# A transformer stack's score cells issued as two 64-column matmul tiles in place of one of 128 columns

## The chip, the cores and the metric

The kernel runs on one core of a Trainium2 chip. Five engines work side by side, each in its own program order, and meet through semaphores: TensorE (PE; its weight loads are listed apart as PEld), VectorE (DVE), ScalarE (ACT), GpSimd (POOL) and SyncE (SP), which issues the DMAs. TensorE multiplies a stationary operand, loaded first, by a moving one that streams through, and writes to PSUM, eight banks of 128 partitions by 512 float32. Its array can be addressed in tiles, by a `tile_position` of row and column. The metric is the device time of one execution in microseconds, the median of the runs shown.

## What is computed

Two rounds of attention and MLP over one sequence of 2048 positions and width 512, the same weights in both rounds, each with a layer norm ahead and a residual behind:

```
x = x + attention(layernorm(x))     # 32 heads of 16
x = x + mlp(layernorm(x))           # 512 -> 1792 -> 512, gelu
x = x + attention(layernorm(x))
x = x + mlp(layernorm(x))

attention: q, k, v = x @ wqkv
           p = softmax(q @ k.T / 4)           # 2048 x 2048 for each head
           (p @ v) @ wo
mlp:       gelu(x @ w1 + b1) @ w2 + b2
```

The inputs and weights are bfloat16.

## The kernel before

**Cells.** The scores are computed transposed, keys on the partitions. One score cell is 128 keys by 512 query columns: K is the stationary operand, 32 rows of it (two heads of 16) by 128 keys, and the queries are the moving one, 32 rows by 512, masked so that one head's rows count. Each cell has a row group `a` of the array (rows 32a to 32a+31) and fills one PSUM bank. There are 4096 cells over both layers. In the profile they are the matmuls of line 1598, `ps<-qp,kt 32*128 32x512`: 32 rows by 128 columns of stationary operand. `qp` holds the masked queries, `kt` K.

**Groups.** `scores` (line 1817) sends cells in groups. Two slots of PSUM banks take turns, `SLOTS = ((0, 1, 2), (3, 4))` with bank 5 (`THIRD`) joined to the second later on. In most of the program a group is three cells of different row groups: two for ACT and a third for DVE (`join`, `trade`, `attach`). A group waits until ACT (semaphore `s_act`) has read the slot's two banks, and its third cell until DVE (`s_dve`) has read its own.

**What reads them.** ACT takes the exponential of the two cells in one instruction of 128x1024 (line 2234, `exps`), to the probability tiles `pt` or to buffers lent for them (`kt`, `v`, `q`). DVE does the third cell by an exponent trick (line 1867, `dfirst`): one multiply-add to 16-bit integers; POOL (line 2097, `shift`) adds constants to them for two more copies, and the three copies enter the value product with weighted copies of V (`vc`).

**Columns.** All other matmuls of weight (`quads`, line 715, for the projections and the MLP; `pvs`, line 2301, for probabilities times values) use tiles of all 128 rows by a strip of 32 columns, four strips side by side; in the profile they read `128*32` and `128*17`. Each set of four is called a round here. PE thus goes back and forth between groups of scores on row tiles and runs of rounds on column tiles.

**The order** of each engine's work is fixed when the program is built: `_Sched` runs the kernel's generators against a table of costs (`MM`, 0.213 us for a round or a group, `SW`, 0.107 us for a change between the two shapes) and appends operations to each engine's list. It fits as many column rounds between two score groups as these costs say PE has time for, and fillers (lines 1586 and 2309) where PE would stand idle. `_Prog.group` (line 275) writes an operation's list of functions with its waits ahead and one semaphore increment on the last.

Of the kernel before, what the change touches and what calls it, by code (L numbers as in the profile page):

```python
# [704 lines left out]
class _Plan:  # L705
# [883 lines left out]
    def score(self, cell, qs, bank):  # L1589

        T = self.T
        pi, kt, a = cell
        l, seg, g = self.pas[pi][:3]
        gb = self.heads(seg, g)[0]
        lhsT = T["K"][l][32 * a:32 * a + 32, gb, kt * 128:(kt + 1) * 128]
        rhs = T["QP"][32 * a:32 * a + 32, qs, :]
        o = self.bank(bank)
        return (lambda e: e.matmul(o, lhsT=lhsT, rhs=rhs, start=True, stop=True, tile_position=(32 * a, 0)),  # L1598
                ["K%d.%d.%d" % (l, gb, kt // 4), "QP.%d" % qs] + ["K0.0.0.b"] * ((l, gb) == (0, 0) and kt in (2, 3)))

    def next_act(self, used=()):
# [820 lines left out]
```

## Time and profile before

| | us |
|---|---|
| median of 3 runs | 1374.87 (1374.37 to 1375.13) |
| profiled execution | 1374.89 |
| its span, first to last instruction | 1373.1 |
| PE busy | 1338.8 (98%) |
| PEld busy | 390.1 (28%) |
| ACT busy | 1349.0 (98%) |
| DVE busy | 1261.8 (92%) |
| POOL busy | 802.8 (58%) |

The granted TensorE clock is 1.00 throughout. A row of a group of instructions gives line, engine and operation, output and inputs by the program's names, shape and count, then busy time in us, the mean of one in ns, and the idle time ahead of it with what ended most of it. A row of a stretch in order of time gives start and length in us, then engine, line, operation and how many are merged in it. Matmul ends are modelled and follow one another closely, so the distance of starts tells more than the lengths. PE's shapes are given as rows*columns of the stationary operand, then the moving one.

### The profile page before, as it was taken

What the parts mean: (1) busy time and instruction counts of PE and PEld (TensorE: products, weight loads), DVE (VectorE), ACT (ScalarE), POOL (GpSimd) and SP (SyncE); (2) the same over time, 40 slices, a digit from 0 to 9 for tenths busy, and PEclk for the clock granted to TensorE, in tenths of its full rate; (3) what the DMA queues carried; (4) which work ended last, traced back from release to release, by engine and by line L of the source; (5) the groups of instructions that cost most, each with busy time, mean ns of one, the idle gap of its engine ahead of it and who ended that gap; (6) DMA issues with size and microseconds to landing.
All of it is one profiled execution on the core that took longest, in us unless ns stands there. A gap on an engine that the chain in (4) does not pass through costs nothing.

```text
span 1373.1 us, 42332 instructions
## 1 busy us (share of the span) xinstructions
PE 1338.8 (98%) x18168; PEld 390.1 (28%) x18168; DVE 1261.8 (92%) x2504; ACT 1349.0 (98%) x1385; POOL 802.8 (58%) x1352
## 2 busy tenths in 40 slices
PE   9999999999999999999999999999999999999999
PEld 3222222222222222222222222222222222333446
DVE  8999999989999899998979899999999898999894
ACT  7999999999999999999999999999999999999995
POOL 1367667657665567665626666546656665765461
DMA  5300000123221221112451141100104314201112
GB/s 149 72 2 1 2 2 23 49 75 97 71 43 45 89 83 55 44 51 65 114 109 40 49 128 57 48 17 12 37 24 117 93 40 143 83 14 44 29 34 83
DMA packets 122296, 80.20 MB, mean 58 GB/s; under 512 B 36732, under 2 KB 121084, under 8 KB 122108
## 3 DMA queue, kind: packets, MB, share of 16 engines
q1 hardware_dynamic: 122108, 77.49, 20.6%
q8 instruction: 143, 2.34, 0.7%
q14 instruction: 45, 0.37, 0.1%
HBM read 65.67 MB, written 4.19 MB: 51 GB/s over the span
## 4 chain that ended last, share of the span: by engine, by line
ACT 83%; PE 10%; DVE 6%; DMA 1%; issue 0%
ACT pt L2234 70%; PE ps L715 5%; ACT kt L2234 3%; ACT g L1276 3%; PE ps L1598 3%; ACT v L2234 2%; PE ps L2301 2%; DVE dp L1867 2%; ACT q L2234 2%; DVE kt L1867 1%; ACT L2234 1%; ACT L1276 1%; ACT g L2234 1%; DVE stats L848 0%; DMA wr<-in_B_w_dram 0%; DMA wr<-in_A_wqkv_dram 0%
## 5 line engine op out<-in xcount | busy, mean ns | idle before, releaser
L2234 ACT ACTIVATE pt<-ps 128x1024 bf16<-128x1024 f32 (+1 forms) x1183 | 1142.7, 1176 | 2.0 <-PE ps L1598 1.6
L1598 PE MATMUL ps<-qp,kt 32*128 32x512 bf16 x4096 | 551.5, 384 | 16.6 <-ACT pt L2234 12.2
L2097 POOL INT64_ADD dp<-dp x732 | 440.2, 613 | 204.8 <-DVE dp L1867 123.1
L1867 DVE TENSOR_SCALAR dp<-ps 128x512 uint16<-128x512 f32 x733 | 483.3, 679 | 26.3 <-PE ps L1598 23.4
L1598 PEld LDWEIGHTS ps<-qp,kt 32*128 32x128 bf16 x4096 | 138.4, 91 | 569.7 <-ACT pt L2234 466.7
L2097 POOL INT64_ADD kt<-kt x320 | 190.1, 599 | 174.1 <-DVE kt L1867 93.6
L2301 PE MATMUL ps<-pt,v 128*17 128x512 bf16 (+1 forms) x2758 | 273.9, 359 | 1.4 <-ACT pt L2234 0.7
L1867 DVE TENSOR_SCALAR kt<-ps 128x512 uint16<-128x512 f32 x309 | 207.4, 683 | 23.4 <-PE ps L1598 20.8
L2301 PE MATMUL ps<-dp,vc 128*17 128x512 bf16 (+1 forms) x1652 | 220.7, 357 | 0.6 <-POOL xf L2097 0.4
L2301 PE MATMUL ps<-dp,v 128*17 128x512 bf16 (+1 forms) x826 | 139.1, 357 | 3.4 <-DVE xt L1076 2.4
L2097 POOL INT64_ADD v<-v x155 | 94.1, 611 | 71.7 <-DVE v L1867 35.8
L715 PE MATMUL ps<-xf,wr 128*32 128x512 bf16 (+1 forms) x1888 | 134.6, 366 | 0.5 <-DVE g L1258 0.4
L2301 PE MATMUL ps<-kt,vc 128*17 128x512 bf16 (+1 forms) x766 | 117.6, 340 | 1.0 <-POOL xf L2097 0.3
L1867 DVE TENSOR_SCALAR v<-ps 128x512 uint16<-128x512 f32 x154 | 102.8, 682 | 13.2 <-PE ps L1598 12.8
L715 PE MATMUL ps<-wr,g 128*32 128x512 bf16 x1408 | 108.1, 384 | 0.5 <-DVE dp L1867 0.2
L2301 PEld LDWEIGHTS ps<-pt,v 128*17 128x17 bf16 x2758 | 69.8, 88 | 74.5 <-issue 51.8
L2301 PE MATMUL ps<-kt,v 128*17 128x512 bf16 (+1 forms) x507 | 85.8, 350 | 1.7 <-DVE xt L1076 1.0
L2097 POOL INT64_ADD xf<-xf x78 | 46.5, 596 | 65.5 <-DVE xf L1867 40.3
L1258 DVE TENSOR_SCALAR g<-ps,hb1t 128x512 bf16<-128x512 f32 (+1 forms) x112 | 78.9, 706 | 1.0 <-PE ps L715 1.0
L2301 PEld LDWEIGHTS ps<-dp,vc 128*17 128x17 bf16 x1652 | 56.7, 88 | 42.0 <-issue 24.4
L2234 ACT ACTIVATE kt<-ps 128x1024 bf16<-128x1024 f32 (+1 forms) x60 | 63.4, 1189 | 0.0
L2301 PE MATMUL ps<-v,vc 128*17 128x512 bf16 x308 | 60.8, 381 | 0.0
(124 smaller groups left out, 1425.5 us busy)
## 6 DMA issues: line engine op xcount, KB each, us to landing
wr<-in_B_w_dram SPq DMA_DIRECT2D x174, 256.0 KB, 2.9
wr<-in_A_wqkv_dram SPq DMA_DIRECT2D x24, 256.0 KB, 3.3
x<-in_A_x_dram SPq DMA_DIRECT2D x7, 512.0 KB, 4.3
wr<-in_A_wo_dram SPq DMA_DIRECT2D x10, 256.0 KB, 3.7
kept<-x SPq DMA_DIRECT2D x4, 512.0 KB, 3.1
x<-kept SPq DMA_DIRECT2D x4, 512.0 KB, 4.4
out_dram<-x SPq DMA_DIRECT2D x16, 128.0 KB, 2.5
q<-in_B_w_dram SPq DMA_DIRECT2D x3, 512.0 KB, 4.5
```

The source lines that it names most:

```text
L715: return [lambda e, a=a: e.matmul(out[32 * a:32 * a + 32, :], lhsT=lhsT[:, 32 * a:32 * a + 32], rhs=rhs, start=start, stop=stop, tile_posi ...
L1258: yield _Op("dve", 0.21 + n / 966, lambda e, fc=fc, pb=pb: e.tensor_scalar(T["G"][:, fc, q], pb, T["HB1T"][:, fc:fc + 1], None, op0=ALU.ad ...
L1276: lambda e, g=g: e.activation(out=g, in_=g, func=ACT.Gelu_apprx_tanh), reads=gk, writes=gk, prio=2)
L1598: return (lambda e: e.matmul(o, lhsT=lhsT, rhs=rhs, start=True, stop=True, tile_position=(32 * a, 0)), ["K%d.%d.%d" % (l, gb, kt // 4), "Q ...
L1867: yield _Op("dve", 0.682, lambda e: e.tensor_scalar(u, self.bank(b), E_SCALE, E_BIAS, op0=ALU.mult, op1=ALU.add), reads=["B.%d" % b], writ ...
L2097: op = _Op("pool", PFIX + PWORD * 128 * (hi - lo), lambda e: e.int64_add(dst, src, by * PACKED), reads=reads, writes=writes)
L2234: yield _Op("act", EXPC + 0.4267 * n, lambda e, src=src, dst=dst: e.activation(out=dst, in_=src, func=ACT.Exp, scale=0.25), reads=["B.%d" ...
L2301: op.fns.append(lambda e, o=o, lhsT=q[0][0][m], rhs=q[0][1][:, n * m:n * m + n], a=a, st=st, sp=sp: e.matmul(o, lhsT=lhsT, rhs=rhs, start= ...
```

## The change

Each score cell's matmul of 32 rows by 128 columns is issued as two of 32 rows by 64 columns, one for the first 64 keys and one for the second. Both stream the same 32x512 queries, stand on the same row group, at columns 0 and 64, and write the lower and upper 64 partitions of the same bank. The cell's two matmuls stand one behind the other in the place of the one; the planner's costs are the same and so is its order.

```
     def score(self, cell, qs, bank):
...
         lhsT = T["K"][l][32 * a:32 * a + 32, gb, kt * 128:(kt + 1) * 128]
         rhs = T["QP"][32 * a:32 * a + 32, qs, :]
         o = self.bank(bank)
-        return (lambda e: e.matmul(o, lhsT=lhsT, rhs=rhs, start=True, stop=True, tile_position=(32 * a, 0)),
+        return (lambda e: [e.matmul(o[64 * c:64 * c + 64, :], lhsT=lhsT[:, 64 * c:64 * c + 64], rhs=rhs, start=True, stop=True, tile_position=(32 * a, 64 * c))
+                           for c in range(2)][-1],
                 ["K%d.%d.%d" % (l, gb, kt // 4), "QP.%d" % qs] + ["K0.0.0.b"] * ((l, gb) == (0, 0) and kt in (2, 3)))
```

The lambda returns the second matmul, so a semaphore increment that the cell had goes on that one. Lines below 1598 move down by one.

On PE in the first layer's attention, at the place that the prediction follows in time (413.89 us and on), before (columns x moving columns, count, and the semaphores waited for; `pt`, `dp`, `v` and `xp` hold probabilities, `wr` weights):

```order
2741 L1598 MATMUL ps<-qp,kt 128x512 [waits s_act]
2742 L1598 MATMUL ps<-qp,kt 128x512
2743 L1598 MATMUL ps<-qp,kt 128x512 [waits s_dve]
2744 L715 MATMUL ps<-xf,wr 32x512 x4
2745 L2301 MATMUL ps<-v,vc 17x512 [waits s_pool]
2746 L2301 MATMUL ps<-v,vc 17x512
2747 L2301 MATMUL ps<-dp,vc 17x512 x2
2748 L2301 MATMUL ps<-xp,v 17x512 [waits s_pool,s_dve]
2749 L2301 MATMUL ps<-xp,v 17x512
2750 L2301 MATMUL ps<-dp,vc 17x512 x2
2751 L1598 MATMUL ps<-qp,kt 128x512 [waits s_act]
2752 L1598 MATMUL ps<-qp,kt 128x512 x2
```

The same place on PE now:

```order
3090 L1598 MATMUL ps<-qp,kt 64x512 [waits s_act]
3091 L1598 MATMUL ps<-qp,kt 64x512 x3
3092 L1598 MATMUL ps<-qp,kt 64x512 [waits s_dve]
3093 L1598 MATMUL ps<-qp,kt 64x512
3094 L715 MATMUL ps<-xf,wr 32x512 x4
3095 L2302 MATMUL ps<-v,vc 17x512 [waits s_pool]
3096 L2302 MATMUL ps<-v,vc 17x512
3097 L2302 MATMUL ps<-dp,vc 17x512 x2
3098 L2302 MATMUL ps<-xp,v 17x512 [waits s_pool,s_dve]
3099 L2302 MATMUL ps<-xp,v 17x512
3100 L2302 MATMUL ps<-dp,vc 17x512 x2
3101 L1598 MATMUL ps<-qp,kt 64x512 [waits s_act]
3102 L1598 MATMUL ps<-qp,kt 64x512 x5
```

Three score matmuls have become six, the wait for ACT ahead of the first and that for DVE ahead of the third cell's first half; the twelve column matmuls between, their order and their waits are what they were.

ACT, which waits for these groups (the exponentials, from an earlier place in the first layer's attention), before:

```order
156 L2234 ACTIVATE pt<-ps 128x2x512 [waits s_pe] x6
157 L2234 ACTIVATE pt<-ps 128x1024 [waits s_pe] x8
158 L2234 ACTIVATE pt<-ps 128x2x512 [waits s_pe]
159 L2234 ACTIVATE kt<-ps 128x2x512 [waits s_pe]
160 L2234 ACTIVATE pt<-ps 128x2x512 [waits s_pe] x2
```

And now:

```order
156 L2235 ACTIVATE pt<-ps 128x2x512 [waits s_pe] x6
157 L2235 ACTIVATE pt<-ps 128x1024 [waits s_pe] x8
158 L2235 ACTIVATE pt<-ps 128x2x512 [waits s_pe]
159 L2235 ACTIVATE kt<-ps 128x2x512 [waits s_pe]
160 L2235 ACTIVATE pt<-ps 128x2x512 [waits s_pe] x2
```

Only the line number has moved.

More of the change, by code (lines that the diff above doesn't have):

```diff
@@ L1597, in score @@
         o = self.bank(bank)
-        return (lambda e: e.matmul(o, lhsT=lhsT, rhs=rhs, start=True, stop=True, tile_position=(32 * a, 0)),
+        return (lambda e: [e.matmul(o[64 * c:64 * c + 64, :], lhsT=lhsT[:, 64 * c:64 * c + 64], rhs=rhs, start=True, stop=True, tile_position=(32 * a, 64 * c))
+                           for c in range(2)][-1],
                 ["K%d.%d.%d" % (l, gb, kt // 4), "QP.%d" % qs] + ["K0.0.0.b"] * ((l, gb) == (0, 0) and kt in (2, 3)))
```

## The prediction

> **What bounds the kernel now.** I read the page's busy times and its chain first, then the groups, then one stretch of attention in order of time, on PE and on ACT, and last the durations by line that price the edit.
>
> From the page (busy us, share, instructions; then the chain by engine and by line):
>
> ```profile
> PE 1338.8 (98%) x18168; PEld 390.1 (28%) x18168; DVE 1261.8 (92%) x2504; ACT 1349.0 (98%) x1385; POOL 802.8 (58%) x1352
> ...
> ACT 83%; PE 10%; DVE 6%; DMA 1%; issue 0%
> ...
> L2234 ACT ACTIVATE pt<-ps 128x1024 bf16<-128x1024 f32 (+1 forms) x1183 | 1142.7, 1176 | 2.0 <-PE ps L1598 1.6
> L1598 PE MATMUL ps<-qp,kt 32*128 32x512 bf16 x4096 | 551.5, 384 | 16.6 <-ACT pt L2234 12.2
> ```
>
> Two engines stand at 98%, and the chain runs mostly through ACT's exponentials. PE's busy share says little, because matmuls overlap and their ends are modelled; what PE has to spare must be read from the spacing of its starts. PE in the middle of attention (start, length, count; the first five rows are score groups with the columns' work between them left out):
>
> ```profile
> 408.55 0.39 PE L1598 MATMUL ps<-qp,kt 32*128 32x512 bf16 x3
> ...
> 409.42 0.39 PE L1598 MATMUL ps<-qp,kt 32*128 32x512 bf16 x3
> ...
> 410.29 0.39 PE L1598 MATMUL ps<-qp,kt 32*128 32x512 bf16 x3
> ...
> 411.23 0.39 PE L1598 MATMUL ps<-qp,kt 32*128 32x512 bf16 x3
> ...
> 412.09 0.39 PE L1598 MATMUL ps<-qp,kt 32*128 32x512 bf16 x3
> ...
> 412.99 0.39 PE L1598 MATMUL ps<-qp,kt 32*128 32x512 bf16 x3
> 413.31 0.61 PE L715 MATMUL ps<-xf,wr 128*32 128x512 bf16 x8
> 413.89 0.39 PE L1598 MATMUL ps<-qp,kt 32*128 32x512 bf16 x3
> 414.21 0.40 PE L715 MATMUL ps<-xf,wr 128*32 128x512 bf16 x4
> 414.43 0.38 PE L2301 MATMUL ps<-v,vc 128*17 128x512 bf16 x2
> 414.44 0.38 PE L2301 MATMUL ps<-dp,vc 128*17 128x512 bf16 x2
> 414.65 0.38 PE L2301 MATMUL ps<-xp,v 128*17 128x512 bf16 x2
> 414.66 0.38 PE L2301 MATMUL ps<-dp,vc 128*17 128x512 bf16 x2
> 414.97 0.39 PE L1598 MATMUL ps<-qp,kt 32*128 32x512 bf16 x3
> 415.29 0.39 PE L2301 MATMUL ps<-xp,vc 128*17 128x512 bf16 x2
> 415.30 0.39 PE L2301 MATMUL ps<-pt,v 128*17 128x512 bf16 x2
> 415.72 0.39 PE L1598 MATMUL ps<-qp,kt 32*128 32x512 bf16 x3
> 416.04 0.83 PE L715 MATMUL ps<-xf,wr 128*32 128x512 bf16 x12
> 416.81 0.39 PE L1598 MATMUL ps<-qp,kt 32*128 32x512 bf16 x3
> ```
>
> Three cells go out together, and 0.32 us later (414.97 to 415.29) comes column work, four matmuls side by side in a round of 0.22 us (414.21, 414.43, 414.65). From the last round to the next scores it is again 0.31 to 0.32 (414.66 to 414.97). So each change between the two shapes costs about 0.10 us above a round, and the least a group can take is 0.63 us with one round of columns, 0.85 with two, 1.07 with three. From 408.55 to 416.81 stand nine groups with 19 rounds (two in each of the first six, then three, one and three): least 9 x 0.63 + 10 x 0.22 = 7.87 us, taken 8.26. PE idles 0.39 us, 43 ns per group or 4.7%. That idling sits in four places: 410.29 to 411.23 (0.94, least 0.85), 412.09 to 412.99 and 412.99 to 413.89 (0.90 each), and 414.97 to 415.72 (0.75, least 0.63). There PE waits until ACT frees the slot.
>
> The exponentials that these groups feed (start, length; ACT's rows overlap, so the step is from start to start):
>
> ```profile
> 413.52 1.23 ACT L2234 ACTIVATE pt<-ps 128x1024 bf16<-128x1024 f32 x1
> ...
> 414.42 1.24 ACT L2234 ACTIVATE pt<-ps 128x1024 bf16<-128x1024 f32 x1
> ...
> 415.40 1.18 ACT L2234 ACTIVATE pt<-ps 128x1024 bf16<-128x1024 f32 x1
> ...
> 416.32 2.09 ACT L2234 ACTIVATE pt<-ps 128x1024 bf16<-128x1024 f32 x2
> ```
>
> ACT's own step is 0.90 us (413.52 to 414.42). A score group's matmuls end 0.39 us after it starts, so the scores of 412.99 and 413.89 lay ready 0.14 us before ACT took them, but those of 414.97 ended at 415.36 and ACT started at 415.40: it had been waiting, and its step was 0.98. The second of the last row starts at about 416.32 + 2.09 - 1.18 = 417.23, right behind the scores of 416.81 (ended 417.20): late again. So ACT leads the chain, but with 0.04 to 0.2 us between it and PE, and twice in nine steps PE is already the later one, each time behind a group with three rounds.
>
> **The change, part by part.** Every score group issues six pairs of weight load and matmul in place of three; the cells are 4096, three to a group as in the rows above, so 4096 / 3 = 1365 groups. The order on PE, DVE, ACT, POOL and SP is otherwise as it was, with the same waits at the same places and one increment per group of matmuls as before. No DMA, no wait and no other engine's instruction is added, so the whole cost is PE time. Durations by line (ns: least, median, longest) of the 128-column load and its matmul, of 32-column ones and of 17-column ones, and PE in one window (busy us, count, then PEld):
>
> ```profile
> L1598 PEld LDWEIGHTS ps<-qp,kt x4096: 90/91/94, 11.8 to 1342.8; 32*128 32x128 bf16 x196
> L1598 PE MATMUL ps<-qp,kt x4096: 371/385/386, 11.8 to 1342.8; 32*128 32x512 bf16 x196
> ...
> L715 PEld LDWEIGHTS ps<-xp,wr x512: 92/94/97, 361.1 to 877.4; 128*32 128x32 bf16 x171
> L715 PE MATMUL ps<-xp,wr x512: 379/379/391, 361.1 to 877.6; 128*32 128x512 bf16 x171
> ...
> L2301 PEld LDWEIGHTS ps<-pt,v x2758: 86/88/93, 15.6 to 1345.5; 128*17 128x17 bf16 x197
> L2301 PE MATMUL ps<-pt,v x2758: 272/379/387, 15.6 to 1345.6; 128*17 128x512 bf16 x156, 128*17 128x256 bf16 x41
> ...
> 400.00:420.00 20.00, 8.60 (x66) 2.13 (x66) 1.00 0.15 42
> ```
>
> *Three more pairs.* In the window 66 score loads, 22 groups, cover 2.13 us: 97 ns per group. One load is 91, so the second and third add 6 together, 3 ns each. Three more pairs: 9 ns per group.
>
> *Narrower loads.* A 64-column load isn't in the trace. Between 17 and 32 columns the load goes from 88 to 94 ns, 0.4 per column, and the longest matmul, the one that follows a load it had to wait for, from 387 to 391, against 379 in steady rounds. On that line 128 columns would take 132 ns; they take 91. So the whole-width load is a quicker kind, and 64 columns on the line of the narrow ones take 94 + 32 x 0.4 = 107 ns, 16 more than now; by the matmuls, 391 + 32 x 0.27 = 400 against 385, 15 more. From above: if the loads of the two halves of a row group followed each other, the second would add what a 64-column load shows of itself, 400 - 379 = 21, so 37. From below: the load shows 385 - 379 = 6 ns now, and no more than these 6 can go. I take 17, nearest the two lines.
>
> *Switching between shapes.* There are as many as now, 0.10 us each, and the trace has the same price into scores (0.31) and out of them (0.32) although the shapes differ, so I put this change at nothing; the faster rival below says otherwise.
>
> *Issuing.* A dense run of short matmuls shows that PE can take more instructions than it will be given:
>
> ```profile
> 1357.42 3.23 PE L715 MATMUL ps<-xf,kt 128*32 128x256 bf16 x112
> 1360.48 0.28 PE L715 MATMUL ps<-xf,wr 128*32 128x256 bf16 x4
> ```
>
> 112 pairs start in 3.06 us, 27 ns a pair. A step of 0.9 us will hold six pairs of scores and eight of columns, 14 x 27 = 0.38 us: nothing on the path.
>
> *The sum on PE.* 9 + 17 = 26 ns per group, 35.5 us over 1365 groups; bounds 9 - 6 = 3 ns (4 us) and 9 + 37 = 46 ns (63 us).
>
> *How much of it shows.* PE has 43 ns per group to spare, but not where it is needed. A delay of PE is wiped out when PE next waits for ACT; it costs time when ACT is found waiting before that. In the stretch the last such wait before ACT's late start at 415.40 ends at 413.89. Two groups' extra, 2 x 26 ns, reach that start; the wait before 415.72 hides nothing of what ACT has lost. The groups of 415.72 and 416.81 bring 52 ns more to the start at 417.23. So 0.104 us of 8.26 shows, 1.26%. Over the stretch in which ACT is full (from about 25 to 1300 us) that is 16 us. Starts that had little to spare turn late too, and the groups before and after that stretch add at most 58 x 26 ns = 1.5 us; I take 18 in all. If nothing of it were hidden it would be 35.5. The sum stands against the profiled execution's own 1374.89 us (span 1373.1, 1.8 around it), which is the median of the runs, 1374.87, to within 0.02. Forecast: 1375 + 18 = **1393 us**.
>
> For this case's own range: 9 ns per group (64 columns load as fast as 128), shown at 18 / 35.5, gives 1365 x 9 ns x 0.5 = 6 us; 46 ns per group is more than PE's 43 to spare, and by the same ratio, raised to two thirds, gives 41. That is 1381 to 1416.
>
> One rule of the Trainium skill speaks against this: its page "TensorE: Matmul & The Clock Gate", section "LDWEIGHTS (loading the stationary operand)", says that a load takes its columns divided by 1.2 GHz, whatever the rows. By it halving the columns would shorten each load from 107 to 53 ns, PE would gain 54 - 9 = 45 ns per group, and nothing would be lost. The rows above disagree: 128 columns load in 91 ns, no longer than 32.
>
> **The rivals.**
>
> *The halves take turns (far slower).* The two tiles of a cell lie on the same 32 rows and stream the same queries. If the second's weights could load only after the first's matmul, each group would take another round: 1365 x 215 ns = 293 us and the 35 above, less at most 43 ns per group (59 us) of idling: 1375 + 269 = 1644. Against it: column rounds are four matmuls on the same 128 rows with weights of their own, and a whole round takes 0.22 us (414.21 to 414.43), so tiles that share rows do run together. What no row shows is several row groups with two column strips each. The same page, section "Part 3: Packing small matmuls — row/col tiling", says that a load overlaps running matmuls only when its row group differs; by that rule it would come out like this, but it also tells of sixteen tiles of rows and columns running side by side.
>
> *PE's idling hides all of it (same).* 26 is below 43. If the waits fell before ACT's late starts, or the price were 3 ns, the time would be 1375 to 1377. For it speaks the sum of the idling, against it that ACT waited at 415.40 and 417.23 directly behind groups that had no wait.
>
> *The switch out of scores gets cheaper (faster).* The 0.10 us at each switch may be the array running empty, and a strip of 64 columns may run empty sooner than one of 128. If half of one switch went, 50 ns, PE would gain 50 - 26 = 24 ns per group; the rival turns the sign from 26 ns on. ACT then takes back only what it loses now. By this row it loses some 15 ns per step:
>
> ```profile
> 402.58 27.75 ACT L2234 ACTIVATE pt<-ps 128x1024 bf16<-128x1024 f32 x30
> ```
>
> (27.75 - 1.18) / 29 = 0.916 us against 0.90 unhindered; 1275 us x 0.015 / 0.916 = 21, half of it 10: 1365 us. Against it: 32 rows by 128 columns and 128 by 32 switch at the same price.
>
> **How the numbers follow.** Forecast's case, both halves side by side at 3 to 46 ns per group and partly hidden: 0.81. Hidden or nearly free: 0.08, 1375 to 1377. Cheaper switch: 0.06, around 1365. Halves in turn: 0.05, around 1644. A measurement of this kernel can tell about 0.2%, 2.7 us, from no change. Slower 0.81 + 0.05 = 0.86, same 0.08, faster 0.06. The range takes the first case and the edge of the second, 1377 to 1416; outside it lie the two rare cases, the rest of the hidden one, and a small share of the first beyond its bounds.
>
> **What the profile after would show.** The score line has 8192 matmuls in groups of six, starting some 3 ns apart; their load is near 107 ns and the matmul near 400. From a score group to the next column work it is 0.34 to 0.35 us in place of 0.32, into scores still 0.31. ACT's mean step grows from 0.916 to about 0.93, its idle before the exponentials names the score line more often, and PE's waits for ACT shrink. The forecast is wrong if score to columns stays at 0.32 or falls (load or switch cheaper than thought), if it is near 0.54 (halves in turn), or if it is 0.35 and ACT's step doesn't move (all hidden).

## The result, and the profile after

The changed kernel takes 1387.87 us (median of 3 runs, 1387.74 to 1389.41) against 1374.87 before: 13.0 us more, a ratio of 1.0099 with a 95% interval of 1.0076 to 1.0121. That is slower, inside the stated range and 5 us below the forecast of 1393.

The page of the profile after (busy times, the chain by engine and by line, and the two groups that were shown of before):

```profile
PE 1358.7 (98%) x22264; PEld 418.0 (30%) x22264; DVE 1266.2 (91%) x2504; ACT 1359.9 (98%) x1385; POOL 801.2 (58%) x1352
...
PE 65%; ACT 23%; DVE 10%; issue 0%; DMA 0%; POOL 0%
...
L2235 ACT ACTIVATE pt<-ps 128x1024 bf16<-128x1024 f32 (+1 forms) x1183 | 1146.6, 1092 | 3.6 <-PE ps L1598 2.0
L1598 PE MATMUL ps<-qp,kt 32*64 32x512 bf16 x8192 | 582.8, 398 | 9.8 <-ACT pt L2235 7.1
```

The busy shares have hardly moved, and say nothing of what happened. The chain does: it ran 83% through ACT and 10% through PE, and now runs 23% through ACT and 65% through PE. PE's idle time ahead of scores fell from 16.6 to 9.8 us.

The same place on PE as in the prediction, from the group that was at 412.99 on (start, length, count):

```profile
416.55 0.41 PE L1598 MATMUL ps<-qp,kt 32*64 32x512 bf16 x6
416.89 0.61 PE L715 MATMUL ps<-xf,wr 128*32 128x512 bf16 x8
417.44 0.41 PE L1598 MATMUL ps<-qp,kt 32*64 32x512 bf16 x6
417.78 0.40 PE L715 MATMUL ps<-xf,wr 128*32 128x512 bf16 x4
418.01 0.38 PE L2302 MATMUL ps<-v,vc 128*17 128x512 bf16 x2
418.02 0.38 PE L2302 MATMUL ps<-dp,vc 128*17 128x512 bf16 x2
418.23 0.38 PE L2302 MATMUL ps<-xp,v 128*17 128x512 bf16 x2
418.23 0.38 PE L2302 MATMUL ps<-dp,vc 128*17 128x512 bf16 x2
418.55 0.41 PE L1598 MATMUL ps<-qp,kt 32*64 32x512 bf16 x6
418.89 0.39 PE L2302 MATMUL ps<-xp,vc 128*17 128x512 bf16 x2
418.90 0.39 PE L2302 MATMUL ps<-pt,v 128*17 128x512 bf16 x2
419.21 0.41 PE L1598 MATMUL ps<-qp,kt 32*64 32x512 bf16 x6
419.56 0.83 PE L715 MATMUL ps<-xf,wr 128*32 128x512 bf16 x12
420.32 0.41 PE L1598 MATMUL ps<-qp,kt 32*64 32x512 bf16 x6
```

Six matmuls go out where three did, merged in one row, and the next column work follows after 0.34 to 0.35 us where it was 0.32. Over the 1133 groups of three cells the median from the first score to the next column work (called score to columns below), from the starts in the two traces, is 345 ns now and 321 before; from the last column matmul to the next scores (the way in) it is 309 now and 312 before. So a group costs 21 ns more, 29 us over 1365 groups, of which 13 show. PE's waits have shrunk: 418.55 to 419.21 is 0.66 us, where 414.97 to 415.72 was 0.75. Added up over the traces, the way in above its 312 or 309 ns falls from 23 to 11 us, and score to columns above the least for a group of its size from 27 to 23 us; these 16 us are the part of the 29 that doesn't show.

The exponentials that belong to these groups:

```profile
417.06 1.07 ACT L2235 ACTIVATE pt<-ps 128x1024 bf16<-128x1024 f32 x1
...
417.96 1.09 ACT L2235 ACTIVATE pt<-ps 128x1024 bf16<-128x1024 f32 x1
...
419.00 1.02 ACT L2235 ACTIVATE pt<-ps 128x1024 bf16<-128x1024 f32 x1
...
419.93 1.02 ACT L2235 ACTIVATE pt<-ps 128x1024 bf16<-128x1024 f32 x1
```

Here the two executions must be read by ends, start plus length. Before, the exponentials of this place end at 413.52 + 1.23 = 414.75, 414.42 + 1.24 = 415.66 and 415.40 + 1.18 = 416.58: 0.91 and 0.92 us apart, although the last started 0.98 after the one ahead of it. ACT lost nothing there; the start was late, but its end wasn't: by the lengths of the records the instruction would otherwise have stood in ACT waiting for the one ahead. Now they end at 418.13, 419.05, 420.02 and 420.95: 0.92, 0.97 and 0.93. The one behind the group with three rounds ends some 0.06 us late (982 ns after the one ahead by the trace's unrounded times, against 917), and that is time lost.

The durations of all exponentials to `pt` by line tell how far ahead PE is (ns: least, median, longest), before:

```profile
L2234 ACT ACTIVATE pt<-ps x1183: 1017/1177/1682, 12.2 to 1339.9; 128x1024 bf16<-128x1024 f32 x180, 128x1536 bf16<-128x1536 f32 x18
```

and after:

```profile
L2235 ACT ACTIVATE pt<-ps x1183: 1018/1045/1632, 12.3 to 1352.7; 128x1024 bf16<-128x1024 f32 x180, 128x1536 bf16<-128x1536 f32 x18
```

These rows mix exponentials of 1024 and 1536 columns; the lead is read from those of 1024 alone. Between 1024-column exponentials that follow one another (1100 such pairs in either trace) one that starts after the one ahead has ended takes 1023 to 1025 ns. One that starts more than some 110 ns before that end is longer, the more so the earlier it starts, and its end stays about 917 ns behind the end ahead, the median distance in both kernels. What a record is longer than 1024 ns is therefore called its lead. Half of them had 150 ns or more of it, and now have 21 or less. Before, 148 of the 1100 started more than 935 ns after the one ahead, and 124 of these still ended within 935 ns of its end; now 211 start so late, and only 43 of them end in time. Ends more than 935 ns apart were 24, which lost 2.1 us above 917; now they are 168 and lose 14.3. The difference, 12.2 us, is nearly all of the 13.

Durations by line of the 64-column load and its matmul (ns: least, median, longest):

```profile
L1598 PEld LDWEIGHTS ps<-qp,kt x8192: 101/101/104, 11.8 to 1355.8; 32*64 32x64 bf16 x200
L1598 PE MATMUL ps<-qp,kt x8192: 371/398/400, 11.8 to 1355.8; 32*64 32x512 bf16 x200
```

The load takes 101 ns against 91 for 128 columns, the matmul behind it 398 against 385.

### The profile page after: what moved, and what is told of

It reads as the page before. It is cut to its first block, busy times and chain, and to the rows that moved or that the text cites. A ratio compares the mean times of both kernels' runs of the same rounds, so it can differ in the third digit from the quotient of the medians.

```text
span 1386.1 us, 50524 instructions
## 1 busy us (share of the span) xinstructions
PE 1358.7 (98%) x22264; PEld 418.0 (30%) x22264; DVE 1266.2 (91%) x2504; ACT 1359.9 (98%) x1385; POOL 801.2 (58%) x1352
## 4 chain that ended last, share of the span: by engine, by line
PE 65%; ACT 23%; DVE 10%; issue 0%; DMA 0%; POOL 0%
PE ps L1598 23%; ACT pt L2235 21%; PE ps L715 21%; PE ps L2302 21%; DVE dp L1868 4%; DVE kt L1868 2%; ACT g L1276 1%; DVE xt L1076 1%; DVE stats L848 1%; PE ps L1586 1%; DVE xf L1868 0%; DVE v L1868 0%; ACT kt L2235 0%; DMA xf<-xln 0%; DVE x L1134 0%
## 5 line engine op out<-in xcount | busy, mean ns | idle before, releaser
L1598 PE MATMUL ps<-qp,kt 32*64 32x512 bf16 x8192 | 582.8, 398 | 9.8 <-ACT pt L2235 7.1
L1598 PEld LDWEIGHTS ps<-qp,kt 32*64 32x64 bf16 x8192 | 166.6, 101 | 554.4 <-ACT pt L2235 440.3
L1868 DVE TENSOR_SCALAR kt<-ps 128x512 uint16<-128x512 f32 x309 | 207.8, 683 | 25.7 <-PE ps L1598 21.9
```

The source lines that it names most:

```text
L1598: return (lambda e: [e.matmul(o[64 * c:64 * c + 64, :], lhsT=lhsT[:, 64 * c:64 * c + 64], rhs=rhs, start=True, stop=True, tile_position=(3 ...
L1868: yield _Op("dve", 0.682, lambda e: e.tensor_scalar(u, self.bank(b), E_SCALE, E_BIAS, op0=ALU.mult, op1=ALU.add), reads=["B.%d" % b], writ ...
```

## The experiments

The theory after the result: the change is a price on PE alone, made of a dearer load and of more tiles, and of this price only that part shows which is left when PE's waits for ACT and the lead of the exponentials are used up. Against it stand rivals for the price (it is all in the number of instructions; or in the column strips) and for the way to the end (PE is simply the bound; or DVE's cells carry the delay). The kernel before took 1374.9 to 1375.1 us beside these runs; its own runs there lie between 1374.3 and 1377.7.

### What the price is made of

**One 64-column tile per cell.** From the ninth pass on the second tile is left out:

```
-                           for c in range(2)][-1],
+                           for c in range(1 if pi >= 8 else 2)][-1],
```

> From the ninth pass on a cell issues only its first 64-key tile and leaves the scores of its other 64 keys out (what the bank held before is read in their place), so there are as many tiles as in the kernel before, each with a 64-column load. Theory: the price is two separate terms, about 13 ns per group for the narrower load and 3.3 ns for each more tile. Then from a group's first score matmul to the next column work it is 321 + 13 = 334 ns (0.33 us), and the time is near half of the change's, about 1381 us. Rival: the 64-column load costs nothing of itself and all 24 ns come from the three more pairs, 8 each: 0.32 us and 1375.

Measured: 1378.82 us, 1.0027 times before (1.0016 to 1.0038), 2 us less than the 1381 expected. Score to columns has a median of 335 ns over the groups of three tiles, as expected. Row of that kernel's PE in time:

```profile
420.40 0.41 PE L1598 MATMUL ps<-qp,kt 32*64 32x512 bf16 x3
420.74 0.62 PE L715 MATMUL ps<-xf,wr 128*32 128x512 bf16 x8
```

Three tiles with a narrower load cost 335 against 321 ns: 14 for the load. The other 10 ns of the change are the three tiles more, 3.3 each. The rival that the instructions alone make the price is out.

**Four tiles of 32 columns.**

```
-        return (lambda e: [e.matmul(o[64 * c:64 * c + 64, :], lhsT=lhsT[:, 64 * c:64 * c + 64], rhs=rhs, start=True, stop=True, tile_position=(32 * a, 64 * c))
-                           for c in range(2)][-1],
+        return (lambda e: [e.matmul(o[32 * c:32 * c + 32, :], lhsT=lhsT[:, 32 * c:32 * c + 32], rhs=rhs, start=True, stop=True, tile_position=(32 * a, 32 * c))
+                           for c in range(4)][-1],
```

> Each cell as four tiles of 32 rows by 32 columns. Theory: load 6.5 ns cheaper than with 64 columns (94 against 101), but twelve pairs in place of six at 3.3 ns: score to columns 345 - 6.5 + 20 = 358 ns (0.36 us), 34 ns more per group than before with 3 back on the way in, 47 us on PE, and 1395 to 1405 us. Rival (only the load's width counts): about 0.34 us and 1382. Rival (column strips of one row group take turns when there are four of them): over 0.5 us and above 1600.

Measured: 1397.13 us, 1.0161 (1.0146 to 1.0177), within the time expected; score to columns 351 ns, not 358. The durations by line of this kernel and a group of it on PE in time:

```profile
L1598 PEld LDWEIGHTS ps<-qp,kt x16384: 86/87/92, 11.8 to 1364.7; 32*32 32x32 bf16 x200
L1598 PE MATMUL ps<-qp,kt x16384: 372/385/387, 11.8 to 1364.7; 32*32 32x512 bf16 x200
```

```profile
412.54 0.42 PE L1598 MATMUL ps<-qp,kt 32*32 32x512 bf16 x12
412.89 0.39 PE L2302 MATMUL ps<-dp,vc 128*17 128x512 bf16 x2
```

Twelve matmuls on three row groups and four strips go out in one round, so tiles that share rows don't take turns. The trace's groups of one, two, three and four cells (4, 8, 12 and 16 tiles) take at least 324, 337, 350 and 364 ns: 3.3 ns per tile again. What is left without tiles is 351 - 12 x 3.3 = 311 ns, the same as in the kernel before (321 - 3 x 3.3 = 311). A 32-column load on 32 rows takes 87 ns, not the 94 of the 128-row tiles: that was the error in the expected 358.

**127 columns.** One key short of the whole width, and not split:

```
+        m = 127 if pi >= 8 else 128
-        return (lambda e: e.matmul(o, lhsT=lhsT, rhs=rhs, start=True, stop=True, tile_position=(32 * a, 0)),
+        return (lambda e: e.matmul(o[0:m, :], lhsT=lhsT[:, 0:m], rhs=rhs, start=True, stop=True, tile_position=(32 * a, 0)),
```

> The kernel before, but from the ninth pass on each cell's matmul has 127 columns of keys instead of 128 (the last key of each 128 is left out). Theory: a load of exactly 128 columns is a quicker kind, and the narrower ones lie on one line, 88 ns at 17 columns, 94 at 32, 101 at 64: 127 columns load in about 115 ns or more, score to columns is 0.35 to 0.36 us in place of 0.32, and the time is 1390 to 1412 us. Rival: what makes the load dearer is the split of the array into column strips, not the width of the load: then 127 columns load in 91 ns and the time is 1375.

Measured: 1405.04 us, 1.0221 (1.0204 to 1.0238). Durations by line of this kernel:

```profile
L1599 PEld LDWEIGHTS ps<-qp,kt x4096: 89/128/133, 11.8 to 1372.8; 32*127 32x127 bf16 x189, 32*128 32x128 bf16 x7
L1599 PE MATMUL ps<-qp,kt x4096: 374/426/427, 11.8 to 1372.8; 32*127 32x512 bf16 x189, 32*128 32x512 bf16 x7
```

A load of 127 columns takes 128 ns, one of 128 columns 91. Score to columns is 363 ns. One key less per cell makes the kernel 30 us slower, so the strips are not the cause: a load short of the whole width is. Without tiles (3.3 ns each) the three plain loads leave 311 ns at 32 columns, 325 at 64 and 353 at 127: 0.44 ns per column. The whole-width load leaves 311, as one of 32 would. The Trainium skill's page "TensorE: Matmul & The Clock Gate", section "Weight-path perf modes — Fast Weight Load (FWL) and DoubleRow", tells of a load of exactly 128 weights in four parallel pieces of 32 columns. The runs agree in what can be seen of it, 311 ns for the whole width as for 32 columns and 353 for 127; that the load is made in four pieces no run shows.

**Split along the queries.** The same number of pairs as the change, but each with the whole width:

```
-        return (lambda e: e.matmul(o, lhsT=lhsT, rhs=rhs, start=True, stop=True, tile_position=(32 * a, 0)),
+        return (lambda e: [e.matmul(o[:, 256 * c:256 * c + 256], lhsT=lhsT, rhs=rhs[:, 256 * c:256 * c + 256], start=c == 0, stop=c == 1, tile_position=(32 * a, 0))
+                           for c in range(2)][-1],
```

> Each cell split along the queries instead: two matmuls of 32 rows by 128 columns over 256 queries each, same weights loaded twice, the quick 128-column load kept. Theory: three more pairs cost 10 ns, two short rounds 2 x 109 in place of 215 cost 3, the second load is hidden behind the first half's stream: score to columns 0.33 us, 1381 us. Rival: the second load of a row group waits until the first half's matmul is through, some 90 to 100 ns more per group: 0.42 us and above 1440.

Measured: 1377.56 us, 1.0019 (1.0010 to 1.0029); score to columns 330 ns, and 312 on the way in as before. Twice the instructions cost 9 ns, and the time is 3 us less than expected. No more than these 9 ns being added, the second load hides behind the first half's stream.

### How the price reaches the end

**ACT slower, with and without the change.** One exponential per cell instead of one per two or three:

```
-            yield _Op("act", EXPC + 0.4267 * n, lambda e, src=src, dst=dst: e.activation(
-                out=dst, in_=src, func=ACT.Exp, scale=0.25),
+            yield _Op("act", EXPC + 0.4267 * n, lambda e, src=src, dst=dst, n=n: [e.activation(
+                out=dst[:, j:j + 1, :], in_=src[:, j:j + 1, :], func=ACT.Exp, scale=0.25) for j in range(n)][-1],
```

> The kernel before with each exponential issued as one ACT instruction per cell in place of one per two or three cells; the results are the same. It makes ACT slower by what an instruction costs besides its elements, and PE's spare time longer by as much. From the steps of 0.903 us for 1024 and 1.330 for 1536 elements that is 49 ns per cut, some 70 us over the kernel, of which up to 20 fall where ACT waits today: 1425 to 1445 us. It is the pair of the next one.

> The same edit of the exponentials on the changed kernel. Theory: the change costs only PE time, some 21 ns per group, and shows only where ACT is found waiting for PE; with some 90 ns per group to spare PE is nowhere late, and this kernel is within 3 us of its pair. Rival: the added time reaches the end by another way than ACT's waiting (the third cells that DVE reads, or PE bound by itself): the difference stays near 13 us.

Measured: 1464.83 us (1463.75 to 1465.70) without the split and 1465.56 (1464.09 to 1466.02) with it. The difference is 0.7 us and within the spread; the 13 us are gone. The chain of the kernel without and of the one with the split:

```profile
ACT 96%; PE 3%; DVE 1%; issue 0%; POOL 0%
```

```profile
ACT 93%; PE 6%; DVE 1%; issue 0%; POOL 0%
```

PE's way in above its 312 or 309 ns, added up over the trace, is 110 us without the split and 86 with it: these waits shrink by 25 of the 29 us that the split costs, and that is where they went. ACT sits idle ahead of exponentials for 2.7 us without and 2.9 with the split, so it is hardly ever short of scores, and in this pair the added time doesn't reach the end by any other way. The size of the slowing was missed: 90 us for 1446 instructions more, 62 ns apiece where 49 were expected. The 49 were worked out from distances of starts. By ends 512-column exponentials follow one another by 490 ns in these two traces, and 2 x 490 is 63 more than the 917 of one of 1024.

**ACT quicker, with and without the change.** Exponentials of 448 of the 512 columns, once a buffer has been filled:

```
+            m = 448 if all(r in self.seen for r in run) else 512
+            self.seen.update(run)
...
-                out=dst, in_=src, func=ACT.Exp, scale=0.25),
+                out=dst[:, :, 0:m], in_=src[:, :, 0:m], func=ACT.Exp, scale=0.25),
```

> The kernel before with exponentials that leave out the last 64 query columns of each cell (448 of 512; the probabilities there are those of an earlier cell). ACT's step falls by 0.107 us to about 0.80, so PE has nothing to wait for on ACT. Theory: PE is the next bound, within 5% of ACT's: 1320 to 1350 us. Rival: PE has little to spare anyway, 1365 or more.

> The same edit on the changed kernel. Theory: with PE the only bound nothing of the added time is hidden; the difference to its pair is 1365 groups x 21 ns = 29 us, with 25 to 30 allowed. Rival: the 13 us are all that the change costs on PE (its waits for DVE and for the other operands take up the rest whatever ACT does): a difference of 12 to 18 us.

Measured: 1362.91 us (1361.96 to 1364.01) without the split, 1384.79 (1384.37 to 1386.06) with it: a difference of 21.9 us, between theory and rival and nearer to the theory. The chains, without and with:

```profile
PE 66%; DVE 30%; ACT 1%; DMA 1%; POOL 1%; issue 1%; POOLq 0%
```

```profile
PE 81%; DVE 16%; ACT 1%; issue 1%; POOL 0%
```

The kernel without the split missed its theory (1350 at most) by 13 us and stops short of the rival's 1365. Its way in above 312 ns fell from 23 to 5 us, as if ACT were no bound any more, but score to columns above the least of its size rose from 27 to 34 us, and DVE, which reads a group's third cell, stands in the chain with 30%: PE had less to win than expected. With the split these 34 us are 27, and DVE's share is 16%. The 7 us are what is missing of the 29, of which 22 show; that they were waits for DVE is read from the chain alone.

**The split in one layer.**

```
+        w = 64 if l == 0 else 128
-        return (lambda e: [e.matmul(o[64 * c:64 * c + 64, :], lhsT=lhsT[:, 64 * c:64 * c + 64], rhs=rhs, start=True, stop=True, tile_position=(32 * a, 64 * c))
-                           for c in range(2)][-1],
+        return (lambda e: [e.matmul(o[w * c:w * c + w, :], lhsT=lhsT[:, w * c:w * c + w], rhs=rhs, start=True, stop=True, tile_position=(32 * a, w * c))
+                           for c in range(128 // w)][-1],
```

> The split in the first layer's attention alone; the second layer's cells are one matmul of 128 columns as before. Theory: what shows is decided within a few groups (a delay lasts until PE next waits for ACT), so the layers add up: about half of the 13 us, 1380 to 1383 us. Rival: spare time in one layer makes good for the other, or the last layer alone decides: 1375 to 1377, or 1388.

Measured: 1382.63 us, 1.0059 (1.0044 to 1.0073): 7.7 of the 13 us from half the cells. Of its late ends (more than 935 ns apart) 86 lie in the first 690 us and lose 8.3 us, and 11 lie behind and lose 1.1; in the kernel before there are 12 in each part, which lose 0.8 and 1.4. What the split loses in the first layer stays lost; spare time in the second doesn't make good for it.

**How the share grows with the price.** The runs with the order of before make a series. The PE price is the group's (score to columns plus the way in, less 321 + 312 ns) times 1365, or 1320 groups for 127 columns:

| kernel | ns per group | us on PE | us more in the time | share | late ends on ACT | us lost by them | median length of a 1024-column exponential, ns |
|---|---|---|---|---|---|---|---|
| before | 0 | 0 | 0 | | 24 | 2.1 | 1174 |
| queries | 9 | 12 | 2.6 | 0.21 | 39 | 3.7 | 1098 |
| half | 11 | 15 | 3.9 | 0.26 | 65 | 5.4 | 1073 |
| the change | 21 | 29 | 13.0 | 0.45 | 168 | 14.3 | 1045 |
| quarters | 27 | 37 | 22.2 | 0.60 | 202 | 22.5 | 1032 |
| 127 columns | 39 | 51 | 30.1 | 0.58 | 210 | 31.2 | 1032 |

The last three columns are of those 1100 pairs; a late end is one more than 935 ns behind the end ahead. In every row the time grows as the us lost by late ends do, to within 2 us (for the quarters 22.2 against 22.5 - 2.1 = 20.4). A first price of 9 to 11 ns eats the lead, from 157 ns above the least down to 55, and three quarters of it cost nothing; from 11 to 27 ns per group 18.3 of 22 further us show, from 27 to 39 another 7.9 of 14. Why the last step shows less than the one before it was not pursued.

### Planning anew

**The change with the planner's switch cost raised to what it measures.**

```
-SW = 0.107
+SW = 0.118
```

> The changed kernel with its order planned anew for its prices: the planner's cost of a change of shape SW is 0.118 us in place of 0.107, since the way into scores and out of them now takes 309 + 345 ns in place of 312 + 321. Theory: PE has the same work, but runs of three rounds are put where PE has time, so less shows: 1379 to 1386 us. Rival: with the chain on PE the work itself is the bound and the order changes nothing: 1387 to 1389.

Measured: 1409.65 us, 1.0251 (1.0233 to 1.0268). Both expectations missed, by 21 us and more. The plan gave DVE 1273 cells in place of 1327. The same constant in the kernel before:

> The kernel before, cells unsplit, planned with SW = 0.118. The run with the split and this plan took 1409.65 us. Its plan gives DVE 1273 cells in place of 1327, so 54 more to ACT, and 54 x 0.427 us (a cell's share of an exponential, from the steps of 0.903 and 1.330 us) is 23 us of ACT. Theory: that loss is the plan's and not the split's, ACT is the bound again and hides the split: 1398 to 1409 us. Rival: the split still costs its 13 us in this order: 1395 to 1397.

Measured: 1407.23 us, 1.0234 (1.0219 to 1.0249). The loss is the plan's; the split costs some 2 us in it, hardly more than the spread. Chains, of the kernel before with this plan and of the changed one with it:

```profile
ACT 77%; PE 17%; DVE 4%; DMA 1%; issue 0%
```

```profile
ACT 78%; PE 15%; DVE 4%; DMA 2%; issue 0%
```

With 54 more cells ACT is the bound in both, and again hides the split. The third plan, for the kernel before, with the mean of the way in and out that the rows show:

```
-SW = 0.107
+SW = 0.101
```

> The kernel before planned with SW = 0.101, what the rows show on the mean of the way into scores and out of them (312 - 215 and 321 - 215 ns). Theory: a truer price lets the plan give PE a little more column work between groups, but ACT and PE both stand at 98%, so there is little to win: 1368 to 1380 us. Rival: another order loses by chance of the plan's choices, as the one before did: 1385 or more.

Measured: 1398.42 us, 1.0169 (1.0152 to 1.0186). The rival holds: 1299 cells for DVE, and the 28 more for ACT are, at 0.427 us each, 12 us of the 23. What the other 11 are was not pursued. No run that computes the whole result was faster than the kernel before; whether a plan tuned for the split would bring back the 13 us stays open.

## Why the prediction was right, and where it missed

**What bounds the kernel.** Right that ACT leads with PE close behind; wrong in its detail. The late starts at 415.40 and 417.23 were taken for time that ACT lost to PE, and 0.90 us, from start to start, for ACT's own step. By ends ACT's step is 0.917, and it lost nothing there. The pair with the slower ACT shows it from one side (no cost), the pair with the quicker one from the other (22 us).

**Three more pairs, 9 ns.** Right: 10, from 3.3 ns per tile in groups of 1 to 4 cells.

**Narrower loads, 17 ns.** A little high: 14. The line through 17 and 32 columns was drawn on tiles of 128 rows, whose 32-column load takes 94 ns; on 32 rows it is 87 and the 64-column one 101 where the line gave 107. That the whole-width load is a kind of its own was right, and 127 columns show it. The rule that was weighed there, columns divided by 1.2 GHz in the Trainium skill's page "TensorE: Matmul & The Clock Gate", section "LDWEIGHTS (loading the stationary operand)", does not hold here: 64 columns load slower than 128 (101 against 91 ns), and the slope among plain loads is 0.43 ns per column (87, 101 and 128 ns) where the rule gives 0.83.

**Switching at nothing.** Nearly: the way into scores became 3 ns cheaper.

**The sum, 26 ns and 35.5 us.** Measured 21 and 29.

**How much shows, 18 us or half.** This is the step that failed in its reasoning, though its size came near: 13 us, 0.45 of the price. It counted each late start as a loss that grows by every delay since PE's last wait. The exponentials had a lead of some 150 ns besides, inside ACT, which had to be used up first. In the stretch followed, where 0.104 us was forecast, one exponential now ends some 0.06 late and the next are on time. The share is no constant either, as the series shows (0.21 to 0.60); that half was near is luck, owed to the price lying where the lead is nearly gone.

**The rivals.** The halves don't take turns: six starts, and twelve with quarters, stand in one round; the way out of scores grew by 24 ns per group, not by the 215 of another round. Idling did hide more than half, but not all; at a price of 9 ns it hid four fifths (2.6 of 12 us show). The cheaper switch did not come: the strip of 32 columns leaves the same 311 ns as that of 128. Its price was wrong too: the 15 ns per step that ACT was said to lose were ACT's own, so there were 2 us to win, not 10.

**What the profile would show.** 8192 matmuls in groups of six, 0.34 to 0.35 us, the matmul at 398, ACT's idle ahead of exponentials named by the score line (1.6 to 2.0 us) and PE's waits for ACT down (12.2 to 7.1): as forecast. The load took 101 ns, not 107. ACT's mean step in one long run of exponentials, from start to start, grew from 0.915 to 0.924, and from end to end from 0.917 to 0.920, not to 0.93, by the records of the row of 402.58 before and of this row of the changed kernel:

```profile
405.05 25.08 ACT L2235 ACTIVATE pt<-ps 128x1024 bf16<-128x1024 f32 x27
```

## What to carry to other kernels

Price a PE edit from the spacing of starts between two kinds of work, not from busy shares: a change of 21 ns per group was readable to a few ns. Then read the engine that is fed by its ends, not its starts: a record that is longer than that of an instruction that finds its engine free is lead, and a delay is mostly free until that lead is gone and dear after it. Keep weight loads at the full 128 columns where loads are exposed: one column less cost 30 us here, more than the 22 of splitting every cell in four.

## What the runs showed that was not expected

ACT's rows overlap so that starts run ahead of ends: in a full run starts stand 0.90 us apart, ends 0.917, and each row is some 13 ns longer than the one before it (1.06, 1.07 and 1.09 us at 416.15, 417.06 and 417.96), until a later start resets it. The way from a column round into scores falls from 312 to 309 ns wherever the load is not of the whole width (64, 32 and 127 columns) and stays at 312 in the kernel split along the queries; it follows the kind of load, not the strip. A plan's constant moved up by 10% or down by 6% cost 32 or 23 us, more than the change under study; the cells that the plan shifted from DVE to ACT make, at 0.427 us each, 23 of the 32 us and 12 of the 23, an estimate, and the rest is open.
